# Sums and splits of three weight matrices made on GpSimd, with jobs that keep their own clock

## The chip, the cores and the metric

One core of a Trainium2 chip. The metric is the device time in microseconds of one launch; the time before is the median of three runs.

## What is computed

With x of 2048 rows and 640 columns:

```python
a = einsum("bsd,ed->bse", x, dft_hid_re); b = einsum("bsd,ed->bse", x, dft_hid_im)
A = einsum("ts,bse->bte", dft_seq_re, a) - einsum("ts,bse->bte", dft_seq_im, b)
h = einsum("bsd,df->bsf", x, w1) + b1              # w1: 640 x 1728
B = einsum("bsf,fd->bsd", h * tanh(softplus(h)), w2)   # w2: 1728 x 640
g = sigmoid((x * gate_w).sum(-1))
out = g * A + (1 - g) * B
```

All in float32. In the kernel the hidden-size matrices dft_hid_re and dft_hid_im are `wd_re` and `wd_im`.

## The kernel before

**Arithmetic.** Every float32 operand is split into a high and a low part of type fp32r: a ScalarE copy makes the high part, a VectorE subtraction the low part (`split`). A product of two operands is then three matmuls, high by high, high by low, low by high (`mm3`, all recorded at L98). The large products are done as block products with seven multiplications for eight (sums and differences of blocks, then the products of them), so that each operand is also summed before it is split. All sums, subtractions and splits are recorded in the helpers `tt` (L86) and `copy` (L89), which is why the profile has few lines.

**Stages.** The order of the core's work is: the sequence transform (`sq`, the stationary tiles made from x, the moving ones from `c_re` and `c_im`), the hidden-size transform (`hd`, stationary from `wd_re` and `wd_im`, moving from the intermediate `u` in DRAM), the first dense layer with w1 (`dense_rest`, `dense_quads`, `dense_first`; its activations go to `act` in DRAM), and the second dense layer with w2 (`ou`), where the gate is applied.

**Steps.** The whole is a written-out list of steps. A step has loads of raw tiles, preparations (sum and split of the moving tile), a few matmuls, and what follows on a finished bank. The main loop at the end of the kernel walks over the steps: raw tiles are loaded up to 9 + 7 steps ahead, preparations recorded up to `LEAD` = 7 steps (`LEAD_D` = 6 in the first dense layer) ahead of the matmuls.

**Jobs.** The stationary tiles that aren't needed at the start are made by jobs, along with the gate's row sums, sums of x, and the gating of stored rows. Jobs stand in one list in a fixed order; each has a load and some work, and pauses with `yield` between pieces of it. One job runs at a time. Two estimates steer when the next piece is recorded: `clock["pe"]` advances by 0.2267 us with each 512-column matmul, `clock["dve"]` with each `tt`, and a piece is recorded while VectorE's clock is behind TensorE's plus a slack. If a step needs a job that hasn't run, `need` records all jobs up to it at once. The jobs that the change touches are `top` and `low` of a `Stage` (its kinds: "seq" for x, "hid" for wd, "out" for w2), `quad_job`, `w1_job` and `w1c_job` for w1, and `w2_job` for the rest of w2. Each takes its stationary tiles from a pool of 26 pairs (`W`), its raw tiles from `FX` (4) and `FS` (22), and gives them back.

The program is in the order in which it is recorded: each engine and SyncE, which issues nearly all transfers, works through its own instructions in that order, and waits by semaphore for those of the others.

Of the kernel before, what the change touches and what calls it, by code (L numbers as in the profile page):

```python
# [10 lines left out]
OP = mybir.AluOpType  # L11

S, D, F = 2048, 640, 1728
P = 128
# [3 lines left out]
KD = D // P  # L18
FC = F // P
FR = F - FC * P  # L20
NF = FC + 1
FP = 6
# [5 lines left out]
SLACK, SLACK_UP, SLACK_D, QUIET = -1.0, 2.5, 1.0, 2  # L28
# [4 lines left out]
QUIET_M, D_END = -1, 24  # L33
# [21 lines left out]
def fnet_mish_gate(ctx: ExitStack, tc: tile.TileContext, xn, xt, c_re, c_im, wd_re, wd_im,  # L55
                   w1a, w1b, b1a, b1b, w2, gw, out):
    nc = tc.nc
# [18 lines left out]
    gsc, qsc = ([r[:, t * N:(t + 1) * N].to_broadcast([P, N]) for t in range(TG)] for r in (g_row, q_row))  # L76
    asc = scratch("act", FC) + [[dr.tile([FR, N], F32, name=f"actr_{t}") for t in range(TG)]]

    clock = {"pe": 0.0, "dve": 0.0, "step": 0}

    def f32(t):
        return t.bitcast(F32)

    def tt(o, a, b, op):
        clock["dve"] += 0.14 + 0.54 * a.shape[-1] / N
        nc.vector.tensor_tensor(o, a, b, op=op)  # L86

    def copy(o, a, scale=1.0):
        nc.scalar.activation(o, a, AF.Copy, scale=scale)  # L89

    def split(h, l, src):

        copy(h, src)
        tt(l, src, f32(h), OP.subtract)

    def mm(ps, a, b, start, stop):
        clock["pe"] += MM * ps.shape[-1] / N
# [7 lines left out]
    def part(w, a, b):  # L105
        return w[0][:, a:b], w[1][:, a:b]
# [4 lines left out]
    A2, B2 = slice(0, 2 * P), slice(2 * P, 4 * P)  # L111
# [20 lines left out]
    jobs, loaded, running, done_jobs = [], [], [], set()  # L132

    class Job:
        def __init__(self, key, work, load=lambda: [], w=0, fx=0, fs=0):
            self.key, self.work, self.load, self.w, self.fx, self.fs, self.first = key, work, load, w, fx, fs, 2

    def simple(fn):
        def work(*a):
            fn(*a)  # L140
            return
            yield
        return work

    def fx_load(src, width=D):
        f = FX.get()
        nc.sync.dma_start(f if width == D else f[:, :width], src)
        return f
# [9 lines left out]

    def job_start():
        j, a, _ = loaded.pop(0)  # L160
        running.append((j.key, j.work(*a)))

    def job_go():
        key, work = running[0]
        pause = next(work, None)
        if pause is None:
            running.pop()
            done_jobs.add(key)
        return pause or 0
# [12 lines left out]
    class Stage:  # L182


        def __init__(self, kind, kh, row, neg=False):
            self.kind, self.kh, self.row, self.neg = kind, kh, row, neg
            self.XA, self.XB, self.XT13 = [None] * kh, [None] * kh, [None] * kh
            self.XT2 = [None] * (kh // KD + 1)

    def t2_part(st, k):  # L190
        return part(st.XT2[k // KD], k % KD * P, (k % KD + 1) * P)

    def b_sums(f, g):

        t = FS.get()
        tt(f[:, A2], f[:, B2], f[:, A2], OP.subtract)
        tt(f[:, B2], g[:, GB], f[:, B2], OP.subtract)
        tt(t[:, A2], g[:, GB], f[:, A2], OP.subtract)
        tt(t[:, B2], g[:, GA], t[:, A2], OP.subtract)
        return t  # L200

    def top(st, k, a):
        w = st.XA[k] = st.XA[k] or W.get()
        split(*part(w, 0, 3 * P), a)

    def low(st, k, g, f):
        if st.neg:
            copy(g, g, -1.0)
            yield 1
        t = b_sums(f, g)  # L210
        yield int(st.kind == "out")
        w = st.XB[k] = W.get()
        st.XA[k] = st.XA[k] or W.get()
        st.XT13[k] = W.get()
        if k % KD == 0:
            st.XT2[k // KD] = W.get()
        split(*w, g)
        FX.put(g)
        yield 0
        split(*part(st.XA[k], 3 * P, 5 * P), t[:, B2])  # L220
        split(*part(st.XT13[k], 4 * P, 5 * P), t[:, :P])
        split(*t2_part(st, k), t[:, P:2 * P])
        FS.put(t)
        yield 0
        split(*part(st.XT13[k], 0, 4 * P), f)
        FS.put(f)

    tops = set()

    def stage_jobs(st, order):  # L230
        def do_top(k, g):
            top(st, k, g[:, :3 * P])
            FS.put(g)

        def top_load(k):
            g = FS.get()
            nc.sync.dma_start(g[:, :3 * P], st.row(k)[:, :3 * P])
            return [g]

        for what, k in order:  # L240
            if what == "top":
                jobs.append(Job((st.kind, "top", k), simple(lambda g, k=k: do_top(k, g)),
                                lambda k=k: top_load(k), (st.kind, k) not in tops, fs=1))
            else:
                jobs.append(Job((st.kind, "low", k), lambda g, f, k=k: low(st, k, g, f),
                                lambda k=k: [fx_load(st.row(k + st.kh)), fs_load(st.row(k)[:, P:])],
                                2 + (k % KD == 0) + ((st.kind, k) not in tops), 1, 1))
            tops.add((st.kind, k))

    def c_split(key, f):  # L250
# [384 lines left out]
    WA, W1, W2C, T2B, QW, extra = [None] * FP, [None] * (FC + 1), {}, [None] * 2, [None] * (FP // 2), []  # L635
# [8 lines left out]
    def quad_job(g, l, m):  # L644


        t = FS.get()
        WA[2 * g], WA[2 * g + 1], QW[g] = W.get(), W.get(), W.get()
        split(*WA[2 * g], l)
        split(*WA[2 * g + 1], m)  # L650
        yield 1
        lo, hi = slice(0, P), slice(P, 2 * P)
        for o, u, v in ((0, m[:, lo], l[:, lo]), (1, m[:, hi], m[:, lo]), (2, m[:, hi], t[:, lo]),
                        (3, l[:, hi], t[:, 2 * P:3 * P])):
            tt(t[:, o * P:o * P + P], u, v, OP.subtract)
        FX.put(l, m)
        yield 1
        split(*part(QW[g], 0, 4 * P), t)
        FS.put(t)

    def w1_job(f, ga, gb):
        t = FS.get()
        a, b, c = WA[f], W.get(), W.get()
        if f % KD == 0:
            T2B[f // KD] = W.get()
        split(*part(b, 2 * P, 5 * P), gb[:, 2 * P:])
        yield 1

        tt(ga[:, A2], gb[:, A2], ga[:, A2], OP.subtract)
        tt(gb[:, A2], gb[:, B2], gb[:, A2], OP.subtract)  # L670
        tt(t[:, A2], gb[:, B2], ga[:, A2], OP.subtract)
        tt(t[:, B2], ga[:, B2], t[:, A2], OP.subtract)
        yield 1
        split(*part(b, 0, 2 * P), t[:, B2])
        split(*part(c, 0, 2 * P), ga[:, A2])
        yield 1
        split(*part(c, 2 * P, 4 * P), gb[:, A2])
        split(*part(c, 4 * P, 5 * P), t[:, :P])
        split(*part(T2B[f // KD], f % KD * P, f % KD * P + P), t[:, P:2 * P])
        FS.put(t)  # L680
        FX.put(ga, gb)
        W1[f] = (a, b, c)

    def w1c_job(g):
        W1[FC - 1] = W.get()
        split(*W1[FC - 1], g)
        FX.put(g)

    def w1r_job(g):
# [11 lines left out]

    def w2_job(name, g):
        W2C[name] = W.get()
        split(*W2C[name], g)
        FX.put(g)

    def dense_jobs():
        for _ in range(NL):
            jobs.append(Job("lend", simple(lend), w=1))
        def quad(g):  # L710
            jobs.append(Job(("quad", g), lambda l, m: quad_job(g, l, m),
                            lambda: [fx_load(w1a[2 * g + i]) for i in range(2)], 3, 2, 1))
        quad(0)
        jobs.append(Job("w1c", simple(w1c_job), lambda: [fx_load(w1a[FC - 1])], 1, 1))
        jobs.append(Job("w1r", simple(w1r_job), lambda: [fx_load(w1b, KD * FR)], 1, 1))
        quad(1)
        quad(2)
        for f in range(FP):
            jobs.append(Job(("w1", f), lambda a, b, f=f: w1_job(f, a, b),
                            lambda f=f: [fx_load(w1a[f]), fx_load(w1a[f + FP])], 2 + (f % KD == 0), 2))  # L720

    def x_split(key, f):
        r = X[key] = R.get()
# [386 lines left out]
    KH = KS // 2  # L1110
    seq = Stage("seq", KH, lambda k: xn[k])
# [30 lines left out]
    aq_jobs()  # L1142
    yg_jobs(2, 3)
    stage_jobs(fin, [("top", 0), ("low", 0), ("top", 1), ("top", 2), ("low", 1), ("low", 2)] + [("top", k) for k in (3, 4, 5)])
    jobs.append(Job("w2c", simple(lambda g: w2_job("c", g)), lambda: [fx_load(w2[(FC - 1) * P:FC * P])], 1, 1))
    jobs.append(Job("w2r", simple(lambda g: w2_job("r", g)), w2r_load, 1, 1))
    stage_jobs(fin, [("low", k) for k in (3, 4, 5)])
    sq[0].first(True)
    sq[1].first()
# [11 lines left out]
    nd = len(steps)  # L1161
# [40 lines left out]
    wait_until = 0  # L1202
    for i in range(n_all):
        clock["step"] = i
        while ready < n_all and ready <= i + (LEAD_D if ready in narrow else LEAD):
            while li < len(loads) and loads[li][0] <= ready + (AHEAD_D if loads[li][0] in narrow else AHEAD):
# [6 lines left out]
                f = RAW[key] = FS.get()  # L1213
# [24 lines left out]
        if not (jobs or loaded or running):  # L1238
            while FX.free:
                FS.put(FX.get()[:, :N])  # L1240
        while clock["dve"] < clock["pe"] + (SLACK_D if nd <= i < nm + D_END else SLACK if ("seq", "low", KH - 1) in done_jobs else SLACK_UP) and i >= wait_until and i not in quiet:
            if running:
                wait_until = i + job_go()
            elif loaded and loaded[0][2] + (5 if i in narrow else 3) <= i and len(W.free) >= loaded[0][0].w:
                job_start()
            else:
                break
# [50 lines left out]
```

## Time and profile before

| | |
|---|---|
| median of 3 runs | 861.7 us (861.66 to 861.98) |
| span of the profiled execution, first to last instruction | 860.5 us |
| TensorE busy, matmuls | 856.2 us, 3766 |
| VectorE busy, instructions | 732.6 us, 1281 |
| ScalarE busy, instructions | 485.6 us, 903 |
| GpSimd busy, instructions | 0.2 us, 4 |

How to read it: the profiled execution's own time is the span of 860.5 us; a run's time has 1.2 us more around it. Matmuls overlap (each is shown as lasting 0.39 us, and a new one begins before the last has ended), so TensorE's busy time alone doesn't tell how full it is. In the rows of groups, `out<-in` are the program's names of tiles: `rh` and `rl` are the high and low parts of moving tiles, `wh` and `wl` those of stationary tiles, `f` and `fx` raw tiles and sums, `ps` PSUM banks. After the shapes stand the count, busy time in all, mean ns of one, and the idle time of the engine just before them with its releaser.

### The profile page before, as it was taken

The page shows a single profiled execution, that of the slowest core. Times are in us where ns is not written, and L with a number is a line of the kernel's source. Part 1 is how long each engine was busy: PE and PEld are TensorE (multiplying, and loading weights), DVE is VectorE, ACT ScalarE, POOL GpSimd, SP SyncE. Part 2 cuts the span into 40 slices and gives each one's busy share as a digit, 9 for nine tenths or more (in the row PEclk, how much of TensorE's full clock was granted, in tenths as well). Part 3 has the DMA queues.
Part 4 walks back from the last instruction along what each step waited for, and adds up shares of the span by engine and source line. Part 5 has one row for each costly group of instructions (what it writes and reads, how often), then busy time and mean ns, then how long its engine had stood idle before and what let it go on. Part 6 is the DMA issues. An engine that isn't in the chain of part 4 may idle for free.

```text
span 860.5 us, 12305 instructions
## 1 busy us (share of the span) xinstructions
PE 856.2 (100%) x3766; PEld 708.4 (82%) x3766; DVE 732.6 (85%) x1281; ACT 485.6 (56%) x903; POOL 0.2 (0%) x4
## 2 busy tenths in 40 slices
PE   9999999999999999999999999999999999999998
PEld 8888888888888888888888888888888888888886
DVE  6999988889879789998998897886578979898993
ACT  6756646464555545657656657764646756542442
POOL 0000000000000000000000000000000000000000
PEclk9999999999999999999999999999999999999999
DMA  9975758885768899898676968879998789485952
GB/s 348 345 255 198 252 164 309 281 287 198 255 234 287 280 343 363 274 316 287 207 261 242 319 197 309 287 231 370 357 377 308 230 283 315 152 289 178 353 185 110
DMA packets 126978, 233.15 MB, mean 271 GB/s; under 512 B 14656, under 2 KB 17216, under 8 KB 126912
## 3 DMA queue, kind: packets, MB, share of 16 engines
q1 hardware_dynamic: 126480, 231.72, 77.9%
q8 instruction: 29, 0.48, 0.2%
q10 hardware_dynamic: 432, 0.66, 0.2%
q14 instruction: 37, 0.30, 0.1%
HBM read 180.13 MB, written 52.18 MB: 270 GB/s over the span
## 4 chain that ended last, share of the span: by engine, by line
PE 100%; ACT 0%; issue 0%
PE ps L98 100%; ACT f L89 0%
## 5 line engine op out<-in xcount | busy, mean ns | idle before, releaser
L98 PE MATMUL ps<-rh,wh 128*128 128x512 f32 (+1 forms) x1062 | 412.1, 389 | 0.0
L98 PE MATMUL ps<-rh,wl 128*128 128x512 f32 x1046 | 405.9, 389 | 0.0
L98 PE MATMUL ps<-rl,wh 128*128 128x512 f32 x1045 | 405.9, 389 | 0.0
L89 ACT ACTIVATE rh<-f 128x512 fp32r<-128x512 f32 x419 | 250.8, 626 | 182.7 <-DVE f L86 101.7
L86 DVE TENSOR_TENSOR rl<-f,rh 128x512 fp32r<-128x512 f32 x417 | 272.5, 686 | 41.3 <-ACT rh L89 40.1
L98 PEld LDWEIGHTS ps<-rh,wh 128*128 128x128 f32 x1062 | 199.5, 188 | 41.6 <-DVE f L86 0.3
L98 PEld LDWEIGHTS ps<-rl,wh 128*128 128x128 f32 x1045 | 196.6, 188 | 40.9
L98 PEld LDWEIGHTS ps<-rh,wl 128*128 128x128 f32 x1046 | 196.3, 188 | 40.7
L86 DVE TENSOR_TENSOR f<-f,f 128x512 f32<-128x512 f32 x305 | 208.4, 688 | 9.6 <-DMA f<-act 2.2
L89 ACT ACTIVATE f<-ps 128x512 f32<-128x512 f32 (+1 forms) x145 | 83.2, 596 | 75.2 <-PE ps L98 66.7
L89 ACT ACTIVATE wh<-f 128x512 fp32r<-128x512 f32 (+3 forms) x173 | 76.7, 484 | 46.7 <-DVE f L86 36.5
L86 DVE TENSOR_TENSOR wl<-f,wh 128x512 fp32r<-128x512 f32 (+3 forms) x172 | 82.3, 512 | 20.5 <-ACT wh L89 20.4
L86 DVE TENSOR_TENSOR f<-ps,f 128x512 f32<-128x512 f32 x100 | 65.5, 683 | 16.9 <-PE ps L98 16.7
L98 PE MATMUL ps<-wh,wh 128*128 128x512 f32 x205 | 79.8, 389 | 0.0
L98 PE MATMUL ps<-wl,wh 128*128 128x512 f32 x200 | 77.8, 389 | 0.0
L98 PE MATMUL ps<-wh,wl 128*128 128x512 f32 x199 | 77.4, 389 | 0.0
L98 PEld LDWEIGHTS ps<-wh,wh 128*128 128x128 f32 x205 | 38.5, 188 | 8.2 <-ACT f L89 0.2
L98 PEld LDWEIGHTS ps<-wl,wh 128*128 128x128 f32 x200 | 37.5, 188 | 7.8
L98 PEld LDWEIGHTS ps<-wh,wl 128*128 128x128 f32 x199 | 37.4, 188 | 7.7
L732 ACT ACTIVATE f<-f,b1s 128x512 f32<-128x512 f32 x36 | 25.5, 721 | 31.5 <-DVE f L86 31.5
L86 DVE TENSOR_TENSOR wl<-fx,wh 128x640 fp32r<-128x640 f32 (+3 forms) x50 | 33.7, 680 | 5.9 <-ACT wh L89 5.9
L89 ACT ACTIVATE wh<-fx 128x640 fp32r<-128x640 f32 (+4 forms) x51 | 31.1, 615 | 5.9 <-DMA fx<-in_xn_dram 3.5
(36 smaller groups left out, 176.5 us busy)
## 6 DMA issues: line engine op xcount, KB each, us to landing
f<-in_c_re_dram SPq DMA_DIRECT2D x128, 256.0 KB, 4.0
f<-in_c_im_dram SPq DMA_DIRECT2D x128, 256.0 KB, 4.5
f<-act SPq DMA_DIRECT2D x87, 256.0 KB, 4.9
f<-u SPq DMA_DIRECT2D x80, 256.0 KB, 5.0
act<-f SPq DMA_DIRECT2D x54, 256.0 KB, 5.1
f<-in_xt_dram SPq DMA_DIRECT2D x49, 256.0 KB, 4.6
u<-f SPq DMA_DIRECT2D x40, 256.0 KB, 3.1
y<-f SPq DMA_DIRECT2D x40, 256.0 KB, 4.9
```

Source lines behind the costliest of these rows:

```text
L86: nc.vector.tensor_tensor(o, a, b, op=op)
L89: nc.scalar.activation(o, a, AF.Copy, scale=scale)
L98: nc.tensor.matmul(ps, a, b, start=start, stop=stop, skip_group_check=True)
L732: nc.scalar.activation(o[rows], src[rows], AF.Mish, bias=b1s[rows, f:f + 1])
```

## The change

Sums and splits of the weights wd, w1 and w2 are recorded on GpSimd. There `gtt` is the two-operand instruction, `gsplit` a split with both halves on GpSimd, and `hsplit` one with the copy on ScalarE and the subtraction on GpSimd. A stage of kind "hid" uses `gtt` and `gsplit`, one of kind "out" `gtt` and `hsplit`; "seq" stays as it was. The negation of `wd_im` goes to GpSimd as well. Jobs that work there are marked `pool=True`; for them the main loop looks at a third estimate, `clock["pool"]`, which GpSimd's instructions advance, and lets them run while it is less than 1 us ahead of TensorE's. The stretches in which no VectorE job is recorded (`quiet`) don't hold them back. Pauses between their pieces become shorter (`yield 0` for `yield 1`; 3 instead of 1 after the sums of w2).

```diff
+    def gtt(o, a, b, op):
+        clock["pool"] += 0.2 + 2.6 / 1200 * a.shape[-1]
+        nc.gpsimd.tensor_tensor(o, a, b, op=op)
+
+    def hsplit(h, l, src):
+
+        copy(h, src)
+        gtt(l, src, f32(h), OP.subtract)
+
+    def gsplit(h, l, src):
+
+        clock["pool"] += 0.2 + 1.1 / 1200 * src.shape[-1]
+        nc.gpsimd.tensor_copy(h, src)
+        gtt(l, src, f32(h), OP.subtract)
...
+            self.tt, self.split = (tt, split) if kind == "seq" else (gtt, hsplit if kind == "out" else gsplit)
...
     def low(st, k, g, f):
+        split = st.split
         if st.neg:
-            copy(g, g, -1.0)
-            yield 1
-        t = b_sums(f, g)
-        yield int(st.kind == "out")
+            clock["pool"] += 0.2 + 1.1 / 1200 * D
+            nc.gpsimd.tensor_scalar(g, g, -1.0, None, op0=OP.mult)
+            yield 0
+        t = b_sums(f, g, st.tt)
+        yield 3 * int(st.kind == "out")
...
-        split(*WA[2 * g], l)
-        split(*WA[2 * g + 1], m)
-        yield 1
+        gsplit(*WA[2 * g], l)
+        gsplit(*WA[2 * g + 1], m)
+        yield 0
...
-        tt(ga[:, A2], gb[:, A2], ga[:, A2], OP.subtract)
+        gtt(ga[:, A2], gb[:, A2], ga[:, A2], OP.subtract)
...
-        split(*W2C[name], g)
+        gsplit(*W2C[name], g)
...
+        def room():
+            ahead = running[0][2] if running else loaded[0][0].pool if loaded else False
+            if ahead:
+                return clock["pool"] < clock["pe"] + 1.0 and i >= wait_until
+            slack = SLACK_D if nd <= i < nm + D_END else SLACK if ("seq", "low", KH - 1) in done_jobs else SLACK_UP
+            return clock["dve"] < clock["pe"] + slack and i >= wait_until and i not in quiet
+
+        clock["pool"] = max(clock["pool"], clock["pe"])
+        while room():
```

More of the change, by code (lines that the diff above doesn't have):

```diff
@@ L77, in fnet_mish_gate @@
     asc = scratch("act", FC) + [[dr.tile([FR, N], F32, name=f"actr_{t}") for t in range(TG)]]
-    clock = {"pe": 0.0, "dve": 0.0, "step": 0}
+    clock = {"pe": 0.0, "dve": 0.0, "pool": 0.0, "step": 0}
     def f32(t):
@@ L134, in fnet_mish_gate, with __init__ @@
     class Job:
-        def __init__(self, key, work, load=lambda: [], w=0, fx=0, fs=0):
+        def __init__(self, key, work, load=lambda: [], w=0, fx=0, fs=0, pool=False):
             self.key, self.work, self.load, self.w, self.fx, self.fs, self.first = key, work, load, w, fx, fs, 2
+            self.pool = pool
     def simple(fn):
@@ L160, in job_start @@
         j, a, _ = loaded.pop(0)
-        running.append((j.key, j.work(*a)))
+        running.append((j.key, j.work(*a), j.pool))
     def job_go():
-        key, work = running[0]
+        key, work, _ = running[0]
         pause = next(work, None)
@@ L191, in t2_part, with b_sums @@
         return part(st.XT2[k // KD], k % KD * P, (k % KD + 1) * P)
-    def b_sums(f, g):
+    def b_sums(f, g, tt):
         t = FS.get()
@@ L203, in top @@
         w = st.XA[k] = st.XA[k] or W.get()
-        split(*part(w, 0, 3 * P), a)
+        st.split(*part(w, 0, 3 * P), a)
     def low(st, k, g, f):
+        split = st.split
         if st.neg:
-            copy(g, g, -1.0)
-            yield 1
-        t = b_sums(f, g)
-        yield int(st.kind == "out")
+            clock["pool"] += 0.2 + 1.1 / 1200 * D
[3 more added lines that the diff above has]
+        yield 3 * int(st.kind == "out")
         w = st.XB[k] = W.get()
@@ L242, in stage_jobs @@
                 jobs.append(Job((st.kind, "top", k), simple(lambda g, k=k: do_top(k, g)),
-                                lambda k=k: top_load(k), (st.kind, k) not in tops, fs=1))
+                                lambda k=k: top_load(k), (st.kind, k) not in tops, fs=1, pool=st.kind != "seq"))
             else:
@@ L246, in stage_jobs @@
                                 lambda k=k: [fx_load(st.row(k + st.kh)), fs_load(st.row(k)[:, P:])],
-                                2 + (k % KD == 0) + ((st.kind, k) not in tops), 1, 1))
+                                2 + (k % KD == 0) + ((st.kind, k) not in tops), 1, 1, pool=st.kind != "seq"))
             tops.add((st.kind, k))
@@ L654, in quad_job @@
                         (3, l[:, hi], t[:, 2 * P:3 * P])):
-            tt(t[:, o * P:o * P + P], u, v, OP.subtract)
+            gtt(t[:, o * P:o * P + P], u, v, OP.subtract)
         FX.put(l, m)
-        yield 1
-        split(*part(QW[g], 0, 4 * P), t)
+        yield 0
+        gsplit(*part(QW[g], 0, 4 * P), t)
         FS.put(t)
@@ L665, in w1_job @@
             T2B[f // KD] = W.get()
-        split(*part(b, 2 * P, 5 * P), gb[:, 2 * P:])
-        yield 1
-        tt(ga[:, A2], gb[:, A2], ga[:, A2], OP.subtract)
[L670 to L679, printed above, removed]
+        gsplit(*part(b, 2 * P, 5 * P), gb[:, 2 * P:])
+        yield 0
+        gtt(ga[:, A2], gb[:, A2], ga[:, A2], OP.subtract)
+        gtt(gb[:, A2], gb[:, B2], gb[:, A2], OP.subtract)
+        gtt(t[:, A2], gb[:, B2], ga[:, A2], OP.subtract)
+        gtt(t[:, B2], ga[:, B2], t[:, A2], OP.subtract)
+        yield 0
+        gsplit(*part(b, 0, 2 * P), t[:, B2])
+        gsplit(*part(c, 0, 2 * P), ga[:, A2])
+        yield 0
+        gsplit(*part(c, 2 * P, 4 * P), gb[:, A2])
+        gsplit(*part(c, 4 * P, 5 * P), t[:, :P])
+        gsplit(*part(T2B[f // KD], f % KD * P, f % KD * P + P), t[:, P:2 * P])
         FS.put(t)
@@ L685, in w1c_job @@
         W1[FC - 1] = W.get()
-        split(*W1[FC - 1], g)
+        gsplit(*W1[FC - 1], g)
         FX.put(g)
@@ L711, in quad @@
             jobs.append(Job(("quad", g), lambda l, m: quad_job(g, l, m),
-                            lambda: [fx_load(w1a[2 * g + i]) for i in range(2)], 3, 2, 1))
+                            lambda: [fx_load(w1a[2 * g + i]) for i in range(2)], 3, 2, 1, pool=True))
         quad(0)
-        jobs.append(Job("w1c", simple(w1c_job), lambda: [fx_load(w1a[FC - 1])], 1, 1))
+        jobs.append(Job("w1c", simple(w1c_job), lambda: [fx_load(w1a[FC - 1])], 1, 1, pool=True))
         jobs.append(Job("w1r", simple(w1r_job), lambda: [fx_load(w1b, KD * FR)], 1, 1))
@@ L719, in dense_jobs @@
             jobs.append(Job(("w1", f), lambda a, b, f=f: w1_job(f, a, b),
-                            lambda f=f: [fx_load(w1a[f]), fx_load(w1a[f + FP])], 2 + (f % KD == 0), 2))
+                            lambda f=f: [fx_load(w1a[f]), fx_load(w1a[f + FP])], 2 + (f % KD == 0), 2, pool=True))
     def x_split(key, f):
@@ L1144, in fnet_mish_gate @@
     stage_jobs(fin, [("top", 0), ("low", 0), ("top", 1), ("top", 2), ("low", 1), ("low", 2)] + [("top", k) for k in (3, 4, 5)])
-    jobs.append(Job("w2c", simple(lambda g: w2_job("c", g)), lambda: [fx_load(w2[(FC - 1) * P:FC * P])], 1, 1))
-    jobs.append(Job("w2r", simple(lambda g: w2_job("r", g)), w2r_load, 1, 1))
+    jobs.append(Job("w2c", simple(lambda g: w2_job("c", g)), lambda: [fx_load(w2[(FC - 1) * P:FC * P])], 1, 1, pool=True))
+    jobs.append(Job("w2r", simple(lambda g: w2_job("r", g)), w2r_load, 1, 1, pool=True))
     stage_jobs(fin, [("low", k) for k in (3, 4, 5)])
@@ L1240, in fnet_mish_gate @@
                 FS.put(FX.get()[:, :N])
-        while clock["dve"] < clock["pe"] + (SLACK_D if nd <= i < nm + D_END else SLACK if ("seq", "low", KH - 1) in done_jobs else SLACK_UP) and i >= wait_until and i not in quiet:
+        def room():
[6 more added lines that the diff above has]
+        while room():
             if running:
```

## The prediction

> **What bounds the kernel now.** I read the page of the profile first: its busy times, its clock row and its chain.
>
> ```profile
> span 860.5 us, 12305 instructions
> PE 856.2 (100%) x3766; PEld 708.4 (82%) x3766; DVE 732.6 (85%) x1281; ACT 485.6 (56%) x903; POOL 0.2 (0%) x4
> ...
> PEclk9999999999999999999999999999999999999999
> ...
> PE 100%; ACT 0%; issue 0%
> ```
>
> TensorE is busy for the whole span, at a granted clock in the top tenth of every slice, and the chain that ended last is TensorE alone. Busy matmuls overlap, so the claim needs a rate and the waits. The rate comes from the windows, the idle time from the view of waits (total, times, longest).
>
> ```profile
> core 0: us, PE busy (x) PEld busy (x) DVE busy (x) ACT busy (x) POOL busy (x), PEclk, DMA share, GB/s
> 20.00:840.00 820.00, 820.00 (x3618) 678.67 (x3617) 713.28 (x1248) 467.60 (x872) 0.00 (x0) 1.00 0.79 273
> 340.00:420.00 80.00, 80.00 (x354) 66.24 (x354) 73.34 (x133) 51.60 (x101) 0.00 (x0) 1.00 0.80 271
> 460.00:560.00 100.00, 100.00 (x443) 82.71 (x442) 84.63 (x153) 67.14 (x133) 0.00 (x0) 1.00 0.79 274
> 640.00:740.00 100.00, 100.00 (x443) 82.81 (x442) 85.95 (x159) 59.37 (x115) 0.00 (x0) 1.00 0.81 281
> ```
>
> ```profile
> PE ps L98 <- PEq L1286: 0.8, 1, 0.8
> PEld ps L98 <- issue: 0.7, 1, 0.7
> PEld ps L98 <- DVE f L86: 0.3, 1, 0.3
> PEld ps L98 <- ACT f L89: 0.2, 1, 0.2
> ```
>
> 820 us hold 3618 matmuls: one every 0.2266 us, and the three shorter stretches have the same rate (80/354 = 0.226, 100/443 = 0.226). The only waits of TensorE and its weight loads for another engine that the view has are 0.3 and 0.2 us. So the whole kernel is one line of matmuls without holes. An engine that feeds it can only be late, never early: what a lighter VectorE or ScalarE can give back is about half a microsecond, under 0.2% of 861.7 us (1.7 us, about what a measurement of this kernel can tell from no change). The change doesn't touch the start or the last stores. The question is therefore only whether it makes a hole.
>
> The engine nearest to making one is VectorE: 73.34 of 80 us in the stretch where the hidden-size weights are made, 84.63 and 85.95 of 100 where w1 and w2 are made.
>
> **What is moved, and its price.** The order of the changed program's instructions shows 194 subtractions gone from VectorE, 78 copies and 5 negations gone from ScalarE, and all 277 on GpSimd, the split copies of w2 staying on ScalarE. The two engines' rows, by form, of the kind that moves, with two that stay:
>
> ```profile
> L86 DVE TENSOR_TENSOR rl<-f,rh 128x512 fp32r<-128x512 f32 x417 | 272.5, 686 | 41.3 <-ACT rh L89 40.1
> L86 DVE TENSOR_TENSOR f<-ps,f 128x512 f32<-128x512 f32 x100 | 65.5, 683 | 16.9 <-PE ps L98 16.7
> L86 DVE TENSOR_TENSOR wl<-f,wh 128x512 fp32r<-128x512 f32 x77 | 51.4, 686 | 15.1 <-ACT wh L89 15.0
> L89 ACT ACTIVATE wh<-f 128x512 fp32r<-128x512 f32 x77 | 46.0, 621 | 18.6 <-DVE f L86 9.5 <-DMA f<-act 6.5 <-DMA f<-xs 2.7
> L86 DVE TENSOR_TENSOR wl<-fx,wh 128x640 fp32r<-128x640 f32 x28 | 22.7, 819 | 2.1 <-ACT wh L89 2.1
> L89 ACT ACTIVATE wh<-fx 128x640 fp32r<-128x640 f32 x28 | 20.2, 730 | 4.5 <-DMA fx<-in_xn_dram 3.5 <-DMA fx<-in_w1a_dram 0.9
> L89 ACT ACTIVATE wh<-f 128x128 fp32r<-128x128 f32 x51 | 12.7, 297 | 0.0
> L86 DVE TENSOR_TENSOR wl<-f,wh 128x128 fp32r<-128x128 f32 x51 | 12.4, 284 | 0.0
> L89 ACT ACTIVATE wh<-f 128x256 fp32r<-128x256 f32 x26 | 10.8, 415 | 28.0 <-DVE f L86 27.0 <-DMA f<-in_xn_dram 1.0
> L86 DVE TENSOR_TENSOR f<-f 128x256 f32<-128x256 f32 x19 | 8.0, 419 | 5.2 <-DMA f<-in_xn_dram 4.2 <-DMA f<-in_w_dram 1.0
> L86 DVE TENSOR_TENSOR wl<-f,wh 128x384 fp32r<-128x384 f32 x18 | 9.8, 552 | 1.8 <-ACT wh L89 1.8
> L89 ACT ACTIVATE wh<-f 128x384 fp32r<-128x384 f32 x18 | 9.1, 515 | 0.0
> L89 ACT ACTIVATE fx<-fx 128x640 f32<-128x640 f32 x5 | 3.6, 727 | 0.0
> L1286 POOL MEMSET const-float32-1.0<- 128x1 f32 x1 | 0.1, 98 | 0.0
> ```
>
> The moved subtractions are 46 of 128 columns, 97 of 256, 17 of 384, 14 of 512 and 20 of 640. At these rows: 46 x 0.284 + 97 x 0.419 + 17 x 0.552 + 14 x 0.686 + 20 x 0.819 = 89.1 us off VectorE. The copies and negations: 22 x 0.297 + 23 x 0.415 + 11 x 0.515 + 8 x 0.621 + 14 x 0.730 + 5 x 0.727 = 40.5 us off ScalarE. Since neither is waited for by TensorE, taking them away is worth nothing by itself.
>
> GpSimd shows only one-column memsets of 98 ns, so the price of the 277 there is bounded. The low end is the rows above: 129.6 us. The high end is what the changed code itself charges them on its own clock, 0.2 + 2.6 n/1200 us for a subtraction of n columns and 0.2 + 1.1 n/1200 for a copy: 194 x 0.2 + 57,216 x 2.6/1200 = 162.8, and 83 x 0.2 + 29,184 x 1.1/1200 = 43.4, together 206.2 us. I take the middle, 168 us, as no row is nearer to one end: most of these subtractions wait for the GpSimd instruction before them, which speaks for the high end, while the charges leave room by design.
>
> GpSimd alone has that time. Placed by the matmuls between which they stand in the changed order, the charges are 71.3 us in the 80 us stretch, 65.3 in the first of 100 us, 56.7 in the second.
>
> **Where a hole can come from.** Nearly all of VectorE's instructions read two SBUF tiles (the rows `rl<-f,rh`, `wl<-f,wh` and their like; the 100 rows `f<-ps,f` read one), and so do GpSimd's. If an instruction of one holds up the other's while both read SBUF, their times add instead of lying side by side. No row of before has GpSimd at work beside VectorE, so the cost of this is bounded too: nothing at one end, all of GpSimd's time at the other. I take the second end as the likelier.
>
> The Trainium skill, SBUF — State Buffer, section "Who interferes with whom", says that a VectorE instruction with two SBUF inputs contends with a GpSimd instruction that reads SBUF, and that whichever starts first keeps the shared read port until it ends. No run so far shows it; by it the sum below stands, and without it the first rival's.
>
> The sum by stretch, with VectorE's instructions counted in the changed order at 272.5/417 = 0.653 us each (busy time per instruction of its largest row):
> - 340 to 420 us: VectorE 88 x 0.653 = 57.5 us (it had 133 instructions). GpSimd 47.2 by the rows, 71.3 by the charges, middle 59.3. Together 116.8 in 80 us: 36.8 too much.
> - 460 to 560 us: 111 x 0.653 = 72.5, GpSimd 42.6 to 65.3, middle 54.0. Together 126.5 in 100 us: 26.5 too much.
> - 640 to 740 us: 99 x 0.653 = 64.6, GpSimd 31.4 to 56.7, middle 44.0. Together 108.6 in 100 us: 8.6 too much.
>
> Against each stands the lead with which the program prepares operands: the subtraction that makes a moving tile stands 38 to 59 matmuls ahead of the first that reads it (medians in the three stretches, counted in the order), 8.6 to 13.4 us. I take 10 us. It is spent before TensorE stops, and won back in the lighter stretches between. So the holes are 36.8 - 10 = 26.8, 26.5 - 10 = 16.5, and 8.6 - 10, so none: 43.3 us. On the median of 861.7 us (the profiled span is 860.5, and 1.2 us lie around it) this gives **905 us**. At the low price: 14.7 + 5.1 + 0 = 19.8, so 881.5. At the high price: 38.8 + 27.8 + 11.3 = 77.9, so 939.6.
>
> Two queues pass such lateness on. On SyncE's queue the 885 transfers are as many as before, but 40 of them now wait for GpSimd, since they load into a tile that it reads last; behind each stand the loads of all moving operands. And 24 ScalarE instructions wait for GpSimd, with the splits of moving tiles behind them. Twelve of VectorE's do.
>
> **The rivals.** *Side by side* (this is the side of no loss): VectorE and GpSimd do not touch each other, and ScalarE's 56% beside VectorE's 85% is the kind of coexistence it would look like. Then GpSimd's 71.3 of 80, 65.3 of 100 and 56.7 of 100 us are all hidden, VectorE is lighter, and TensorE runs as before: 861.7 us. It decides from the share of GpSimd's time that VectorE loses: in the tightest stretch TensorE stops only when 57.5 plus that share of 59.3 us exceeds 80 + 10, at a share over 0.55. Chance 0.17.
>
> *GpSimd late by itself*: no holding up, but its instructions cost 1.5 times the charges. Then the first stretch asks 107 us of it in 80. The weights of the fifth hidden-size row pair are read only 33 matmuls, 7.5 us, after the place where they are made, and another 10 us of lateness go in the lead of the loads that wait for GpSimd: 27 - 17 = 10 us, so 872 us. Against it: most weight tiles are made 20 to 80 us ahead of their first matmul. Chance 0.09.
>
> *Faster*: only through the half microsecond of waits above. Chance 0.01. That the work doesn't move is excluded by the order.
>
> **How the numbers follow.** Taking turns has 0.73, with 881.5 to 939.6 us by price; side by side 0.17; late 0.09. The predicted time is the first's, 905. The range reaches from the side-by-side case to the high price, 861.5 to 940. Over 940 stays what the price could be above the charges. Slower by over 0.2%: 0.73 + 0.09 = 0.82; same 0.17; faster 0.01.
>
> **What would show it.** Right: TensorE waits of tens of microseconds in all, in the stretches of the hidden-size and the w1 weights and next to none after 760 us; VectorE instructions of the unchanged forms longer than 686 ns, or idle before them with nothing that released it, while GpSimd works; GpSimd instructions longer beside VectorE than alone. Wrong: TensorE as full as now with GpSimd 130 to 210 us busy and VectorE's `rl<-f,rh` still at 686 ns. If these stay at 686 and TensorE still waits, behind a transfer or GpSimd, the second rival holds.

## The result and the profile after

The changed kernel takes 888.1 us (median, 887.91 to 888.82) beside 861.84 us for the kernel before in the same measurement: a ratio of 1.0305, 95% interval 1.0290 to 1.0319. It is 26.3 us slower. The profiled execution spans 886.1 us; before it was 860.5.

The page of the changed kernel, its busy times and the chain that ended last:

```profile
span 886.1 us, 12440 instructions
...
PE 866.6 (98%) x3766; PEld 711.9 (80%) x3766; DVE 746.2 (84%) x1087; ACT 454.7 (51%) x820; POOL 277.1 (31%) x281
...
PE 31%; POOL 5%; DMA 2%; ACT 1%; DVE 1%; issue 1%; SPq 0%; ACTq 0%; POOLq 0%
```

VectorE has 194 instructions fewer and is busy 13.6 us longer (746.2 us, 732.6 before). The last line's shares do not sum to the whole, so I use it only to see that the chain no longer lies on TensorE alone. Where the holes (stretches without a matmul) are is seen in the windows, with the columns of the prediction:

```profile
340.00:420.00 80.00, 72.89 (x294) 57.73 (x294) 76.00 (x79) 32.82 (x59) 68.56 (x65) 0.94 0.73 241
420.00:460.00 40.00, 38.54 (x170) 31.59 (x170) 39.20 (x38) 17.65 (x32) 33.29 (x29) 1.00 0.63 208
460.00:560.00 100.00, 96.28 (x414) 78.14 (x413) 94.65 (x122) 56.73 (x103) 58.89 (x62) 0.98 0.78 263
580.00:640.00 60.00, 57.56 (x255) 47.34 (x254) 32.10 (x47) 27.90 (x47) 20.30 (x29) 1.00 0.99 347
640.00:740.00 100.00, 100.00 (x443) 82.84 (x442) 67.23 (x94) 56.84 (x106) 43.33 (x42) 1.00 0.79 278
```

At one matmul every 0.2266 us the 80 us from 340 on had 354 matmuls; now they have 294. The missing 60 are worth 13.6 us. The 100 us from 460 on are short of 29, 6.6 us, and the stretches 420 to 460 and 580 to 640 of 7 and 10, 3.7 us. The stretch of w2, 640 to 740, has its 443. Who ended TensorE's waits, from the view of waits (us, times, longest):

```profile
PEld ps L113 <- DVE rl L86: 14.2, 10, 2.4
PE ps L113 <- DVE rl L86: 10.5, 9, 2.0
PEld ps L113 <- ACT f L89: 2.9, 1, 2.9
PE ps L113 <- ACT f L89: 2.4, 1, 2.4
```

A matmul and its weight load stand in two rows for the same wait, so the rows are not to be added. TensorE's matmuls waited mostly for the low part of a moving tile, `rl`, which is VectorE's: an instruction that the change didn't touch. In the groups by form (busy us, mean ns) these instructions have become longer:

```profile
L86 DVE TENSOR_TENSOR rl<-f,rh 128x512 fp32r<-128x512 f32 x417 | 321.5, 804 | 62.4 <-ACT rh L89 60.4 <-DMA act<-f 1.3
L86 DVE TENSOR_TENSOR f<-f,f 128x512 f32<-128x512 f32 x315 | 239.6, 765 | 13.5 <-DMA f<-y 4.0 <-DMA f<-act 2.4 <-DMA xs<-f 1.0
L86 DVE TENSOR_TENSOR f<-ps,f 128x512 f32<-128x512 f32 x99 | 64.7, 682 | 28.0 <-PE ps L113 27.9
L86 DVE TENSOR_TENSOR wl<-f,wh 128x512 fp32r<-128x512 f32 x68 | 55.9, 839 | 8.3 <-ACT wh L89 8.2
L86 DVE TENSOR_TENSOR f<-f,fx 128x512 f32<-128x512 f32 x28 | 24.3, 878 | 7.3 <-ACT f L751 6.7 <-DMA out_dram<-f 0.6
L89 ACT ACTIVATE rh<-f 128x512 fp32r<-128x512 f32 x416 | 248.2, 626 | 229.7 <-DVE f L86 136.1 <-PE ps L113 74.6 <-DMA f<-act 7.7
L98 POOL TENSOR_TENSOR f<-fx,f 128x256 f32<-128x256 f32 x39 | 37.6, 972 | 3.9 <-DMA xs<-f 1.0 <-DMA act<-f 0.7
L98 POOL TENSOR_TENSOR wl<-fx,wh 128x640 fp32r<-128x640 f32 x20 | 36.3, 1814 | 7.1 <-ACT wh L89 6.0
```

`rl<-f,rh` went from 686 to 804 ns on the mean of all 417, and the other 512-column forms with two SBUF operands that are shown went up as well. The form that reads one operand from PSUM stayed at 682, and ScalarE's copy stayed at 626. By these four slower rows VectorE lost 417 x 0.118 + 315 x 0.077 + 68 x 0.153 + 28 x 0.193 = 89 us, while the 194 moved instructions had taken 89.1 off it (by the prediction's sum): nothing was gained there.

### The profile page after: what moved, and what is told of

It is laid out like the page before. It is cut to its first block, busy times and chain, and to the rows that moved or that the text cites. A ratio compares the mean times of both kernels' runs of the same rounds, so it can differ in the third digit from the quotient of the medians.

```text
span 886.1 us, 12440 instructions
## 1 busy us (share of the span) xinstructions
PE 866.6 (98%) x3766; PEld 711.9 (80%) x3766; DVE 746.2 (84%) x1087; ACT 454.7 (51%) x820; POOL 277.1 (31%) x281
## 5 line engine op out<-in xcount | busy, mean ns | idle before, releaser
L113 PE MATMUL ps<-rl,wh 128*128 128x512 f32 x1050 | 411.6, 393 | 10.5 <-DVE rl L86 10.5
L113 PE MATMUL ps<-rh,wl 128*128 128x512 f32 x1053 | 411.1, 391 | 0.0
L86 DVE TENSOR_TENSOR rl<-f,rh 128x512 fp32r<-128x512 f32 x417 | 321.5, 804 | 62.4 <-ACT rh L89 60.4
L86 DVE TENSOR_TENSOR f<-f,f 128x512 f32<-128x512 f32 x317 | 240.8, 765 | 13.5 <-DMA f<-y 4.0
L227 POOL TENSOR_SCALAR fx<-fx 128x640 f32<-128x640 f32 x5 | 10.9, 2170 | 336.9 <-DMA fx<-in_wd_im_dram 336.9
L98 POOL TENSOR_TENSOR wl<-f,wh 128x128 fp32r<-128x128 f32 (+3 forms) x76 | 78.2, 1040 | 78.0 <-DMA y<-f 71.8
L89 ACT ACTIVATE wh<-f 128x512 fp32r<-128x512 f32 (+3 forms) x132 | 63.7, 516 | 45.1 <-DVE f L86 30.6
L86 DVE TENSOR_TENSOR wl<-f,wh 128x512 fp32r<-128x512 f32 (+3 forms) x101 | 66.8, 688 | 8.3 <-ACT wh L89 8.2
L98 POOL TENSOR_TENSOR wl<-fx,wh 128x640 fp32r<-128x640 f32 (+2 forms) x38 | 56.7, 1492 | 8.5 <-ACT wh L89 6.0
L98 POOL TENSOR_TENSOR f<-fx,f 128x256 f32<-128x256 f32 (+1 forms) x45 | 42.6, 956 | 4.1 <-DMA xs<-f 1.0
```

Source lines behind the costliest of these rows:

```text
L98: nc.gpsimd.tensor_tensor(o, a, b, op=op)
L113: nc.tensor.matmul(ps, a, b, start=start, stop=stop, skip_group_check=True)
L227: nc.gpsimd.tensor_scalar(g, g, -1.0, None, op0=OP.mult)
```

## The experiments

Two theories stood against each other. *Taking turns*: VectorE and GpSimd hold each other up when both read SBUF, wholly (as the prediction's sum has it) or by part. *Late by itself*: GpSimd doesn't disturb VectorE, but what it makes comes late.

**GpSimd work that nobody needs.** To the kernel before, GpSimd instructions on tiles of their own are added, started by the gate's last instruction at 229 us. No engine waits for them. They read a constant, one column over and over, in place of two tiles.

```diff
+        if clock["pe"] > 227 and not started:
+            started.append(nc.gpsimd.tensor_copy(own[:, :KS], gates[:, 2 * KS:]))
+            for _ in range(130):
+                nc.gpsimd.tensor_tensor(own, one, one, op=OP.subtract)
```

> The kernel before, all its work in its place, plus 130 GpSimd subtractions of 256 columns on tiles of their own, back to back from about 229 us on; nothing waits for them. In the changed kernel the shortest subtraction of this size took 0.73 us, so they ask 95 us of GpSimd. 'Late by itself' (GpSimd and VectorE don't touch; TensorE waits only because what GpSimd makes comes late): 861.7 us, since nobody reads these tiles. 'Taking turns, all of the time' (the sum of the prediction): VectorE is busy 82 of the 100 us from 240 to 340, so 82 + 95 - 100 - 10 = 67 us more, about 929. 'Slowing each other by part', with the share read from the changed kernel (VectorE lost about 90 us over some 240 us in which both were busy, 0.37 us per us): GpSimd needs about 140 us, VectorE loses 0.37 x 130 = 48 us in it, 115 + 48 - 140 - 10 = 13 us more, about 875.

For the next two, the loop is 240 times `nc.gpsimd.tensor_copy(own, one)`, and 240 times `nc.gpsimd.memset(own, 0.0)`.

> The same with 240 GpSimd copies of 256 columns (one tile read in place of two; shortest in the changed kernel 0.39 us, so 94 us). 'Late by itself': 861.7. 'Taking turns': as with the subtractions, about 928. 'By part': if VectorE loses the same share beside a copy, about 875; if one read takes half as much from it as two, about 862 to 865.

> The same with 240 GpSimd memsets of 256 columns, which read nothing. If VectorE's loss comes from reading at the same time, as the prediction has it: 861.7, and VectorE's 512-column subtractions stay at 686 ns. If any GpSimd work beside VectorE slows it, they get longer and the time rises, to at most the figure of the copies. 'Late by itself': 861.7.

Measured: subtractions 887.38 us (ratio 1.0296, 1.0279 to 1.0313), copies 877.89 us (1.0184, 1.0169 to 1.0200), memsets 861.89 us (1.0000, 0.9991 to 1.0010). The instructions' own rows (duration ns least/median/greatest) for GpSimd's work and, from 235 to 330 us, for VectorE's subtraction beside it, first of the run with subtractions, then copies, then memsets:

```profile
L1244 POOL TENSOR_TENSOR own<-const-float32-1.0 x130: 611/942/1167, 228.9 to 359.4; 128x256 f32<-128x256 f32 x130
...
L89 DVE TENSOR_TENSOR rl<-f,rh x49: 676/1097/1101, 234.6 to 328.2; 128x512 fp32r<-128x512 f32 x49
```

```profile
L1244 POOL COPY own<-const-float32-1.0 x240: 400/738/941, 229.7 to 411.4; 128x256 f32<-128x256 f32 x120
...
L89 DVE TENSOR_TENSOR rl<-f,rh x57: 676/877/900, 234.6 to 326.4; 128x512 fp32r<-128x512 f32 x57
```

```profile
L1244 POOL MEMSET own<- x240: 311/312/318, 228.9 to 317.3; 128x256 f32 x120
...
L89 DVE TENSOR_TENSOR rl<-f,rh x60: 681/686/693, 234.8 to 329.1; 128x512 fp32r<-128x512 f32 x60
```

And two rows by form of the run with subtractions, same stretch, one for the subtraction with two SBUF operands and one for an instruction with one of its operands in PSUM, with a window of it:

```profile
L89 DVE TENSOR_TENSOR rl<-f,rh 128x512 fp32r<-128x512 f32 x49 | 50.9, 1081 | 0.0
L89 DVE TENSOR_TENSOR f<-ps,f 128x512 f32<-128x512 f32 x4 | 2.5, 677 | 0.0
...
250.00:300.00 50.00, 43.46 (x181) 34.69 (x181) 49.45 (x52) 19.61 (x36) 46.17 (x50) 0.97 0.58 174
```

This settles the main question. With nobody waiting for GpSimd, 130 subtractions cost 25.4 us: 'late by itself' isn't needed for a loss of this size. Reading is what counts: a memset, which reads nothing, leaves VectorE at 686 ns; a copy (256 columns read) takes it to 877, 0.19 more; a subtraction (512 read) to 1097, 0.41 more. That is about 0.8 ns for each column that GpSimd reads. VectorE's instructions with one operand in PSUM (only four in this stretch) keep 677.

How the turns go is seen in single instructions (start and duration in us), two pairs of the changed kernel and one of the run with subtractions:

```profile
490.51 1.90 POOL L98 TENSOR_TENSOR wl<-fx,wh 128x640 fp32r<-128x640 f32 x1
490.90 2.06 DVE L86 TENSOR_TENSOR wl<-f,wh 128x512 fp32r<-128x512 f32 x1
...
350.60 1.34 POOL L98 TENSOR_TENSOR wl<-f,wh 128x384 fp32r<-128x384 f32 x1
350.99 1.50 DVE L86 TENSOR_TENSOR rl<-f,rh 128x512 fp32r<-128x512 f32 x1
```

```profile
261.77 0.94 POOL L1244 TENSOR_TENSOR own<-const-float32-1.0 128x256 f32<-128x256 f32 x1
262.16 1.10 DVE L89 TENSOR_TENSOR rl<-f,rh 128x512 fp32r<-128x512 f32 x1
262.79 0.94 POOL L1244 TENSOR_TENSOR own<-const-float32-1.0 128x256 f32<-128x256 f32 x1
```

VectorE's instruction, which starts 0.39 us after GpSimd's, ends 0.55 us after that one's end, whether GpSimd took 0.94, 1.34 or 1.90 us. GpSimd's next one in turn ends 0.47 us after VectorE's. The two add up to the 1.02 us from one pair to the next (the 50 us window has 52 VectorE instructions and 50 subtractions of GpSimd). So, by these ends, the main part of each instruction waits until the other's is done, and only a little of each lies beside the other: 0.69 - 0.55 and 0.61 - 0.47, 0.14 us. In the changed kernel a column that GpSimd's subtractions read costs more, (2.06 - 0.69)/1280 = 1.07 ns.

The time of the run follows: VectorE's 110.7 us of work between 228.9 and 359.4 us in the kernel before, with 130 x 0.41 = 53 lost, make 33 us too much for 130.5, 23 after a lead of 10: 885, and 887 were measured. All of the 0.611 us of each subtraction on top would have made 911 by the same sum (the 929 of the expectation took 0.73 us each).

The Trainium skill's page SBUF — State Buffer, section "Who interferes with whom", has both conditions as the runs show them: two SBUF inputs against a GpSimd instruction that reads (1097 ns), none against one that only writes (686). Its exclusive lock, under which the second one is blocked until the first has finished, agrees with the pairs above (0.55 us after GpSimd's end, however long that one takes), but for the 0.14 us of each instruction that are not held up.

**How much is absorbed.** The same with 30 and with 65 subtractions.

> The kernel before plus 30 in place of 130 of the separate GpSimd subtractions. In the run with 130 VectorE's subtraction of 512 columns took 1.10 us beside one of them and 0.686 without: 0.41 us lost on each. 30 of them cost VectorE 12 us in some 31 us of which 18% (5.5 us) were spare: 7 us late, less than the lead of about 10 us that the prediction's sum takes. 'By part' with that lead: 861.7 to 862.5. If there is no such lead: about 868.

> The same with 65. 27 us lost, 12 spare: 15 late, 10 of it in the lead, so 5 us of hole, and the matmuls after a hole run at half pace for a while: 866 to 869. Without a lead: about 877.

Measured: 862.48 us with 30 (ratio 1.0006, 0.9997 to 1.0016) and 871.85 with 65 (1.0111, 1.0095 to 1.0128). The windows over GpSimd's work, of 30 and of 65:

```profile
229.00:260.00 31.00, 31.00 (x139) 25.67 (x138) 30.76 (x31) 14.65 (x26) 27.72 (x30) 1.00 0.66 208
```

```profile
229.00:298.00 69.00, 64.21 (x273) 51.68 (x271) 68.31 (x71) 27.48 (x48) 60.54 (x65) 0.98 0.65 196
```

With 30, VectorE has no time left (30.76 of 31 us), and TensorE still doesn't notice: the lead swallows it. With 65 it is used up and 10.1 us are lost, more than the 4 to 7 expected. So there is a threshold. VectorE's work of the kernel before in the same stretches (23.55 and 56.55 us) and 0.41 us for each subtraction make it 5 us late with 30, 14 with 65 and, as above, 33 with 130; 0, 10.1 and 25.4 us were lost. By this the lead is some 4 to 8 us, less than the 10 of the prediction.

**The parts of the change.** Each weight matrix alone on GpSimd, the others made as before.

```diff
# wd alone: quad_job, w1_job, w1c_job, w2_job and their jobs as before, and
+            self.tt, self.split = (gtt, gsplit) if kind == "hid" else (tt, split)
# w2 alone: the jobs of w1 as before, and
+            self.tt, self.split = (gtt, hsplit) if kind == "out" else (tt, split)
# w1 alone: Stage and w2_job as before
+            self.tt, self.split = tt, split
```

> The change for the hidden-size weights alone (85 of the 277 instructions on GpSimd, 63 us by the charges); w1 and w2 as before. By the holes of TensorE in the changed kernel between 340 and 460 us, about 15 us over the matmuls' pace, of which the first w1 jobs have a part: 'slowing each other by part' gives 872 to 877. 'Late by itself' gives the same order of size, but with TensorE's waits ended by GpSimd or by transfers that wait for it.

> The change for w1 alone (128 instructions, 87 us by the charges). By the holes of the changed kernel from 460 to 600 us, about 9 us, and the part of w1's first jobs before: 'by part' gives 871 to 876. The three parts should add up to the whole, 26 us, within about 5.

> The change for w2 alone (64 instructions on GpSimd, 57 us by the charges, copies on ScalarE). The prediction's sum has no hole here (108.6 of 100 us at the middle price, against a lead of 10 us), and the changed kernel shows 0.7 us: 862 to 863 by either form of taking turns. If the holes in the other stages only hid one here, up to 870.

Measured: wd alone 874.33 us (ratio 1.0143, 1.0127 to 1.0159), w1 alone 872.96 (1.0127, 1.0112 to 1.0142), w2 alone 863.66 (1.0022, 1.0013 to 1.0032), with 861.79 before. The losses are 12.5, 11.2 and 1.9 us, 25.6 together against 26.3 for the whole: each stage pays for itself. w2 alone lost 0.7 us more than the upper end of what was expected.

**Copies and negations back on ScalarE**, first all 83, then only the 5 negations of `wd_im`:

```diff
# all copies
     def gsplit(h, l, src):
-        clock["pool"] += 0.2 + 1.1 / 1200 * src.shape[-1]
-        nc.gpsimd.tensor_copy(h, src)
+        copy(h, src)
# both kernels
-            nc.gpsimd.tensor_scalar(g, g, -1.0, None, op0=OP.mult)
+            copy(g, g, -1.0)
```

> The changed kernel with the 78 copies and 5 negations back on ScalarE; only the 194 subtractions stay on GpSimd. At the shortest times seen in the changed kernel that takes about 40 of 199 us off GpSimd. 'Taking turns' in either form: the loss shrinks at least in that proportion, 26.3 x 159/199 = 21, so 883 or less. If the negations of 640 columns (2.2 us each) and the copies did most of the harm: near 865. 'Late by itself': GpSimd is less late, but each subtraction now waits for ScalarE; 870 to 890.

> The changed kernel with only the 5 negations of 640 columns back on ScalarE. On GpSimd they took 2.2 us each, and the VectorE instructions beside them 2.06 in place of 0.69. 'By part': 5 x 1.4 = 7 us less lost by VectorE, all in the stretch where holes are, so 5 to 8 us faster than the changed kernel, 880 to 883. If the added wait of the sums on GpSimd for ScalarE costs as much as in the run with all copies on ScalarE: 886 to 890.

Measured: all back 891.06 us (ratio 1.0341, 1.0325 to 1.0356), the negations back 884.07 (1.0263, 1.0246 to 1.0280). The first was a miss: I expected 883 or less, and taking work off GpSimd made it slower than the changed kernel. VectorE did lose less (`rl<-f,rh` at 782 ns, 804 in the changed kernel), but the view of waits of that run shows a new one:

```profile
POOL wl L98 <- ACT wh L89: 196.4, 32, 76.8
...
ACT wh L89 <- POOL f L98: 38.5, 14, 5.4
```

ScalarE now waits 38.5 us for sums that GpSimd makes (7.3 us in the changed kernel), and in its queue the copies for the moving tiles stand behind. The chain of a weight tile goes back and forth between the two engines. I read the extra 3 us as this wait; no run took it away alone. The negations back on ScalarE won 4 of the 5 to 8 us expected, and hardly through VectorE, whose `rl<-f,rh` stayed at 799 ns; where the 4 us come from is not shown.

The suspicion against the negations rested on 2.2 us for each and on VectorE instructions of 2.06 us. So 100 of the kind on 256 columns, in the same place as the other separate work (the loop is `nc.gpsimd.tensor_scalar(own, one, -1.0, None, op0=OP.mult)`):

> The kernel before plus 100 separate GpSimd instructions of the negation's kind (a tensor and a constant) on 256 columns. One tile is read, as by the copy, which took 0.19 us off VectorE for 256 columns. If the loss goes by columns read: VectorE's subtraction of 512 at about 0.88 us, as beside the copies. If this kind holds VectorE up for its whole time, as the 2.06 us in the changed kernel look like: over 1.2 us.

```profile
L1244 POOL TENSOR_SCALAR own<-const-float32-1.0 x100: 847/1308/1406, 229.1 to 347.5; 128x256 f32<-128x256 f32 x100
...
L89 DVE TENSOR_TENSOR rl<-f,rh x58: 676/679/883, 235.7 to 329.6; 128x512 fp32r<-128x512 f32 x58
```

The one time measured is 864.44 us. The instruction is slow by itself (847 ns at least, where a copy takes 400), but it takes no more from a VectorE instruction than a copy: 883 ns at most. More than half of the 58 are not slowed at all (median 679), where about 880 was expected of them. So the loss does not go by how long GpSimd is at work.

The 2.06 us have another neighbour than the expectation thought: in the changed kernel's trace every VectorE instruction of 2 us or more lies beside a GpSimd subtraction of 640 columns, as in the first pair shown above. The suspicion against the negations was a misreading.

**GpSimd's clock slower**, so that the same 277 instructions lie further apart:

```diff
-        clock["pool"] += 0.2 + 2.6 / 1200 * a.shape[-1]
+        clock["pool"] += 0.28 + 3.64 / 1200 * a.shape[-1]
-        clock["pool"] += 0.2 + 1.1 / 1200 * src.shape[-1]
+        clock["pool"] += 0.28 + 1.54 / 1200 * src.shape[-1]
```

> The changed kernel with GpSimd's charges on its clock 1.4 times as high (0.28 + 3.64 n/1200 and 0.28 + 1.54 n/1200 us), about what its instructions took beside VectorE, so that the same 277 instructions are recorded further apart. 'By part': VectorE loses the same in all, but less of it in one stretch, and some of it where it has time to spare: fewer holes, 870 to 882. 'Late by itself': weights come later still and TensorE waits more, 890 or over.

Measured: 892.80 us (ratio 1.0362, 1.0342 to 1.0383). A miss for my theory, and in the range that I had given to the rival. Lines of it, by form, by windows and, from 640 to 664 us, by waits:

```profile
L86 DVE TENSOR_TENSOR rl<-f,rh 128x512 fp32r<-128x512 f32 x419 | 319.5, 798 | 54.0 <-ACT rh L89 53.3
```

```profile
640.00:740.00 100.00, 94.67 (x417) 77.73 (x416) 65.67 (x94) 53.93 (x99) 36.06 (x35) 1.00 0.84 286
...
640.00:664.00 24.00, 18.67 (x82) 14.78 (x81) 11.87 (x20) 12.13 (x22) 0.00 (x0) 1.00 1.00 324
```

```profile
ACT rh L89 <- DMA f<-in_xt_dram: 4.6, 2, 3.5
ACT wh L89 <- DMA f<-xs: 4.4, 1, 4.4
PE ps L113 <- ACT f L89: 3.1, 1, 3.1
PE ps L113 <- ACT ps L89: 2.2, 1, 2.2
```

VectorE's loss per instruction is the same (798 ns, 804 in the changed kernel), as expected. But TensorE has holes in a stretch that had none, 417 matmuls in place of 443. They stand in its first 24 us (82 where 106 have room), in which GpSimd does nothing at all, so they are not made by two engines that read at the same time. TensorE waits twice for ScalarE there, and ScalarE stood for two loads before, of `xs` and of x, while the DMA engines are busy for the whole stretch (share 1.00). So the order of the jobs has a price of its own, through the transfers. Why these loads came late there, GpSimd's earlier lateness or the order itself, was not tried and stays open.

## Why the prediction was right, and where its sizes were off

**What bounds the kernel**: right. TensorE had nothing to gain, and what it lost are holes in its line of matmuls and slow matmuls after some of them.

**The mechanism**: right. The likeliest case was that the two engines' reads of SBUF hold each other up, with VectorE the late one. That their times add holds for a pair that meets, but for 0.14 us of each. VectorE's unchanged forms lengthened, the form with one operand in PSUM did not, and the added work that nobody waits for made the same loss. *Side by side* fell with 1.0305; *late by itself* fell as the main cause with the 25.4 us of the unneeded subtractions. It has a share at the edges, where an engine in order waits for GpSimd: shown as a wait (38.5 us in the run with the copies back), not priced alone.

**The sign, the place and the range**: right; 888.1 lies between 861.5 and 940. Holes stand at wd and w1, and almost none at w2, as the sum by stretch had it: 26.8, 16.5 and none forecast, 12.5, 11.2 and 1.9 measured by the parts.

**The size**: 43.3 us forecast, 26.3 measured. Terms were off in both directions, so it is in part luck that the forecast came as near as it did.
- *GpSimd's price*, the middle of 168 us between the rows of the other engines and the charges, was too low. Each of the 277 at the shortest time that its kind and size has in the changed kernel makes 202 us (for instance 0.73 us for its sums `f<-fx,f` of 256 columns; the code charges 0.755, VectorE's row has 0.419). So the charges, 206.2 us, were right; beside VectorE GpSimd was busy 277.1. At that price the prediction's own sum gives about 939 us.
- *The share of GpSimd's time that VectorE loses* was taken as all of it. Measured in whole: 89 us of 202, less than half. A pair that meets loses more than that on VectorE: 0.41 us on a subtraction of 0.611 us, two thirds; 0.19 on a copy of 0.400, half. The rest is what overlaps in such a pair, and GpSimd's work beside an idle VectorE or one that reads PSUM. This is the term that made the forecast too high.
- *The sum by stretch* is too coarse for the holes that there are. From 340 to 420 us the two rows below lose 45 x 0.379 + 28 x 0.366 = 27 us, where the sum has 59.3; 57.5 + 27 is under 90, so it would have no hole there, yet 60 matmuls are missing. VectorE had 39.38 of 40 us from 340 to 380 before, so the average over 80 us hides the tightest part; and from 420 to 460, a stretch that the sum leaves out, it had 38.91 of 40 and GpSimd was still at work (33.29 us). The lead could not be won back there. How the 26.3 us divide among these was not measured.

```profile
L86 DVE TENSOR_TENSOR rl<-f,rh 128x512 fp32r<-128x512 f32 x45 | 45.6, 1065 | 3.3 <-ACT rh L89 3.3
L86 DVE TENSOR_TENSOR f<-f,f 128x512 f32<-128x512 f32 x28 | 29.5, 1054 | 0.7
```

- *What a hole costs* was left out. After some holes the granted clock is near half for a while:

```profile
362.20:364.50 2.30, 0.34 (x2) 0.00 (x0) 2.27 (x4) 1.03 (x3) 1.12 (x1) 1.00 0.30 109
365.60:369.00 3.40, 3.40 (x11) 2.66 (x10) 3.33 (x7) 2.24 (x6) 0.00 (x0) 0.57 0.88 264
399.80:406.60 6.80, 6.45 (x16) 5.11 (x17) 6.80 (x8) 3.19 (x6) 6.64 (x6) 0.54 0.47 122
532.90:536.30 3.40, 3.40 (x11) 2.66 (x10) 3.40 (x5) 2.58 (x6) 3.19 (x5) 0.58 0.75 217
```

The first line is a hole of 2.3 us, still at full clock; the next is what follows it, at 0.57. At 0.2266 us those three slow stretches, 13.6 us, would hold 60 matmuls; the table counts 38 starts or overlaps. The missing 22 are worth about 5 us. How much of that comes on top of the lateness isn't shown, since VectorE catches up while TensorE is slow: wd alone lost 12.5 us at a mean granted clock of 1.00.

**The lead of 10 us**: there is one, of some 4 to 8 us by the separate subtractions. 30 of them cost nothing that can be told, 65 cost 10.1 us.

## What to carry to other kernels

Where TensorE's matmuls stand without a hole, moving work from one of the other engines to another has next to nothing to win (half a microsecond here), however idle the engine that takes it; look for the hole first. Before moving elementwise work to GpSimd beside a busy VectorE, count the columns that GpSimd will read from SBUF: in these runs each cost VectorE 0.8 to 1.1 ns when its instruction had two SBUF operands, and nothing when GpSimd only wrote or VectorE read PSUM. To tell a disturbance from a late result, add the same work on tiles that nobody reads.

## What was not expected of the hardware

When both read SBUF, VectorE and GpSimd take turns instruction by instruction, and only some 0.14 us of each lie side by side: a VectorE subtraction of 512 columns and a GpSimd one of 256 take 1.02 us as a pair, against 0.69 + 0.61 = 1.30. A VectorE instruction of 0.69 us could so take 2.06. GpSimd's multiplication of a tensor by a constant took 847 ns for 256 columns, twice the copy's 400, and slowed VectorE's instructions no more than the copy did. And no matmul waited longer than 2.4 us in the changed kernel, but after some of the holes there were three stretches of 3.4 to 6.8 us at little over half the full clock.
